# Root sums of the second gated layer moved between two products of a unit, and the next pass's input sums queued behind the global tile's first piece

## The chip, the cores and the metric

The kernel runs on one core of one Trainium2 chip. The metric is the device time in microseconds (us), of one execution from start to end. Three runs of the kernel before took 894.93, 897.28 and 897.6 us.

## What is computed

2304 tokens (4 batches of 512 local and 32 global tokens) go through attention, a feed-forward layer with ELU, and a gated feed-forward layer behind an RMS norm:

```python
x = np.ascontiguousarray(attn_out.transpose(0, 2, 1, 3)).reshape(B * S, H * D)
x = _moe_ref(x=x, **moe_kwargs)               # elu(x @ w_in) @ w_out
return _moe2_ref(x=x, **moe2_kwargs)

rms = np.sqrt(np.mean(x * x, axis=-1, keepdims=True) + 1e-06)
xn = x / rms * rms_g
g = xn @ w_gate
silu = g * (1.0 / (1.0 + np.exp(-g)))
val = xn @ w_val
return (silu * val @ w_out).astype(np.float32)
```

Model width 512, hidden width 1536 in the gated layer. The change concerns the gated layer and the end of the layer before it.

## The kernel before, in words

**Number format.** A large product takes both operands as a rounded high part and the rest (tile element 0 and 1), and sums three matmuls of the parts (`PASSES`). So every operand has a split: ScalarE (ACT) casts the high part, VectorE (DVE) subtracts it from the source. L625 and L626 do this for a group of weights (`split`), L691 and L692 for an input set (`x_split`), L828 and L829 for a gated result (`halves`).

**Who sets the order.** TensorE (PE) runs its instructions in the order of the program text. ACT and DVE are ordered by a scheduler; each then works its queue in that order. `behind(mark)` tells the scheduler to place what stands inside it after the two instructions that `mark` holds at that moment, one on ACT and one on DVE.

**End of the first layer.** `moe_block(3, slot3)` runs 16 steps j. A step has 12 matmuls h (L132), for j from 10 on also the products of the 128 global tokens (`hg` L701, transposes `egt` L708, `yg` L717), and 12 matmuls y (L153). From j=10 on `second_slot(j - 10)` prepares the gated layer's first pass: `y_square`, `y_root` (one matmul with a matrix of ones, L660; on ACT a table load and the square root, L662; on DVE the reciprocal, L663), `y_norm` (L670), `y_sums` (L676, L689) and `x_split`. h, hg and the two `ms` of this pass take turns in the two PSUM buffers of the pool `hps`.

**The gated layer.** Two passes k of 1024 tokens, each with 6 units i of hidden columns. The gate and value products of a unit go by a scheme with seven products in place of eight: positions 0 to 6, each for gate (z=0) and value (z=1), 6 matmuls per half, so 12 per position (L818). Positions 0, 2, 4, 5 add up in `A` (two buffers of `hps`), 1 and 3 with 6 in `Q` (two buffers of `aps`). ACT copies `A` out (L1006, L1019, L1025), DVE adds `Q` to the copies (`add_to`, L833). The results go into output products o (L824), 12 matmuls for one hidden block.

After a unit of pass 0 stands work for later: after unit 0 `g_root` (the root for the global tokens: a matmul `msg` L767, ACT's root L768, and their normed and split input `xg`, `xd`), after units 2 and 3 `y_root(1, ...)`, which take a buffer of `aps` as `Q` does.

**Between the passes.** Pass 0 ends with 12 output products of 12 matmuls (loop z over `js`). Between them lies the global tile in six pieces: `tile_products` (24 matmuls `pg`, L788; then silu on ACT, L793, and the product `pe` on DVE, L794), `tile_turn` (PE transposes `pe` to `pgt`, L800; ACT and DVE split it, L802 and L803), `tile_out` (6 matmuls `og`, L810). The same stretch makes the next pass's input: three wide sums (`y_sums`, L676), a fourth (L689) and seven input sets (`x_split`).

Of the kernel before, what the change touches and what calls it, by code (L numbers as in the profile page):

```python
# [7 lines left out]
F32 = mybir.dt.float32  # L8
# [4 lines left out]
AF = mybir.ActivationFunctionType  # L13
ALU = mybir.AluOpType
# [7 lines left out]
P = 128  # L22
# [11 lines left out]
def f(ap):  # L34
    return ap.bitcast(F32)
# [7 lines left out]
def fused_kernel(ctx: ExitStack, tc: tile.TileContext, kq, vl, gkq, gv, w_in, w_out, w_gate, w_val, w_o2, rms_g, consts, out):  # L43
# [533 lines left out]
        fetch()  # L577

    wraws, n_fetch, todo, groups = [], [0], [], {}
    n_split = [0]  # L580

    todo += [("w", q) for q in range(3)] + [("o", 0), ("o", 1)]
    for q in range(3, 54):
# [26 lines left out]
    def split(n=1):  # L610
        for _ in range(n):
            if n_split[0] >= len(todo):
                return
            kind, i = todo[n_split[0]]
            n_split[0] += 1
            raw = wraws.pop(0)
            if kind == "w":
                t = wpool.tile([P, 8, 2, P], F32R, tag="w", name="wS")
                raw = raw.rearrange("p (a n) -> p a n", a=8)
                groups[i] = t  # L620
            else:
                t = wpool.tile([P, 2, 2, 512], F32R, tag="w", name="wB")
                raw = raw.rearrange("p (a n) -> p a n", a=2)
                Wo[2 * i], Wo[2 * i + 1] = t[:, 0], t[:, 1]
            nc.scalar.copy(t[:, :, 0, :], raw)  # L625
            nc.vector.tensor_tensor(out=t[:, :, 1, :], in0=raw, in1=f(t[:, :, 0, :]), op=ALU.subtract)  # L626
            fetch()

    def need(q):
# [25 lines left out]

    def y_root(k, h):
        if k < 2:
            pool, tag = (aps, "att") if k else (hps, "h")
            ms = pool.tile([P, 512], F32, tag=tag, name="ms")
            nc.tensor.matmul(ms, bpools["ones"], rs_[k, h], start=True, stop=True)  # L660
            rs = stg.tile([P, 512], F32, tag="stg", name="rs")
            nc.scalar.activation(rs, ms, AF.Sqrt, bias=eps, scale=1.0 / DM)  # L662
            nc.vector.reciprocal(rs, rs)  # L663
            rs_[k, h] = rs
# [65 lines left out]
    def second_slot(i):  # L730

        if i == 0:
            y_square(0, 0)
        elif i == 1:
            y_root(0, 0)
            y_square(0, 1)
        elif i == 2:
            y_root(0, 1)
            y_norm(0, 0)
        elif i == 3:  # L740
            y_norm(0, 1)
            y_sums(0)
            split()
        elif i == 4:
            x_split(0, ("B11", "B21", "T2"))
        elif i == 5:
            split()
            x_split(0, ("T1", "T3"))
            with behind(mark):
                x_split(0, ("T4", "B22"))  # L750

    gg = {}

# [25 lines left out]
    def tile_products(i):  # L779
        ps = hps.tile([P, 512], F32, tag="h", name="pg")  # L780
        for h in range(2):
            need(21 + 2 * i + h + 1)
            w = groups[21 + 2 * i + h].rearrange("p (s a) l n -> p s a l n", a=2)
            xs_ = (xg[:, 0:2], xd if h else xg[:, 2:4])
            for m in range(2):
                for c in range(2):
                    for z, (xl, wl) in enumerate(PASSES):
                        nc.tensor.matmul(ps[:, 256 * h:256 * h + 256], xs_[m][:, c, xl, :], w[:, 2 * m:2 * m + 2, c, wl, :],  # L788
                                         start=(m == 0 and c == 0 and z == 0), stop=(m == 1 and c == 1 and z == 2))
        pv = ps.rearrange("p (h s n) -> p h s n", h=2, s=2)  # L790
        e = moe.tile([P, 512], F32, tag="e", name="pe", bufs=2)
        e2 = e[:, :256].rearrange("p (h n) -> p h n", h=2)
        nc.scalar.activation(e2, pv[:, :, 0, :], AF.Silu)  # L793
        nc.vector.tensor_tensor(out=e2, in0=e2, in1=pv[:, :, 1, :], op=ALU.mult)  # L794
        return e

    def tile_turn(i, e):
# [198 lines left out]
    for k in range(2):  # L996
# [3 lines left out]
        for i in range(6):  # L1000
            j1, j2 = 4 * (i // 2) + i % 2, 4 * (i // 2) + i % 2 + 2
            A = [hps.tile([P, 512], F32, tag="h", name="A") for _ in range(2)]
            t1, t2, t3 = (moe.tile([P, 2, 512], F32, tag=f"xT{z}", name=f"t{z + 1}") for z in range(3))
            for z in range(2):
                product(A[z], k, i, 0, z)
                nc.scalar.copy(t1[:, z], A[z])  # L1006
            Q = [aps.tile([P, 512], F32, tag="att", name="Q") for _ in range(2)]
            for z in range(2):
                product(Q[z], k, i, 1, z)
                add_to(t1[:, z], Q[z])  # L1010
                if z == 0:
                    nc.scalar.activation(t1[:, 0], t1[:, 0], AF.Silu)
            nc.vector.tensor_tensor(out=t1[:, 0], in0=t1[:, 0], in1=t1[:, 1], op=ALU.mult)
            p11 = halves(t1[:, 0])
            if late is not None:
                o_mm(os1, *late, False, False)
            for z in range(2):
                product(A[z], k, i, 2, z, False)
                nc.scalar.copy(t2[:, z], A[z])  # L1019
            Q = [aps.tile([P, 512], F32, tag="att", name="Q") for _ in range(2)]  # L1020
            for z in range(2):
                product(Q[z], k, i, 3, z)
            for z in range(2):
                product(A[z], k, i, 4, z, False)
                nc.scalar.copy(t3[:, z], A[z])  # L1025
                add_to(t3[:, z], Q[z])
                if z == 0:
                    nc.scalar.activation(t3[:, 0], t3[:, 0], AF.Silu)
            nc.vector.tensor_tensor(out=p2[:, slot2(j2), :], in0=t3[:, 0], in1=t3[:, 1], op=ALU.mult)
            o_mm(os1, p11, j1, i == 0, False)  # L1030
            for z in range(2):
                product(A[z], k, i, 5, z, False)
            e = moe.tile([P, 512], F32, tag="e", name="s", bufs=2)
            nc.scalar.activation(e, A[0], AF.Silu)
            nc.vector.tensor_tensor(out=e, in0=e, in1=A[1], op=ALU.mult)
            p21 = halves(e)
            for z in range(2):
                product(Q[z], k, i, 6, z, False)
                add_to(t2[:, z], Q[z])
                if z == 0:  # L1040
                    nc.scalar.activation(t2[:, 0], t2[:, 0], AF.Silu)
            kept = p2[:, slot2(j1), :] if i < 5 else t2[:, 0]
            nc.vector.tensor_tensor(out=kept, in0=t2[:, 0], in1=t2[:, 1], op=ALU.mult)
            late = (p21, j2)
            if k == 0 and i == 0:
                g_root(*yg)
                y_load(1)
            elif i == 1:
                y_square(k + 1, 0)
            elif i == 2:  # L1050
                y_root(k + 1, 0)
                y_square(k + 1, 1)
            elif i == 3:
                y_root(k + 1, 1)
                y_norm(k + 1, 0)
            elif i == 4:
                y_norm(k + 1, 1)
        js = [2, 0, 9, 3, 1, 6, 4, 7, 5, 10, 8, 11]
        second = lambda j: kept if j == 9 else p2[:, slot2(j), :]
# [3 lines left out]
        copied = store_out(os1, 8 * k, more)  # L1063
        ps.append(halves(second(js[1])))
        if k == 0:
            need(22)
            with behind(mark):
                pe = tile_products(0)
        os2 = [aps.tile([P, 512], F32, tag="att", name="o4") for _ in range(2)] + [yps.tile([P, 512], F32, tag=f"y{t}", name="o5") for t in range(2)]
        if k == 0:  # L1070
            og = yps.tile([P, 512], F32, tag="y3", name="og")
            with behind(mark):
                y_sums(1)
            pg = None
            for z, j in enumerate(js):
                o_mm(os2, ps.pop(0) if ps else halves(second(j)), j, z == 0, z == 11)
                if z % 2 == 0:
                    if z:
                        tile_out(og, z // 2 - 1, pg)
                    pg = tile_turn(z // 2, pe)  # L1080
                elif z < 11:
                    pe = tile_products(z // 2 + 1)
                if z % 3 == 1 and z < 9:
                    with behind(mark):
                        x_split(1, XSETS[z - 1:z + 2])
            tile_out(og, 5, pg)
            store_out(os2, 4)
            store_out([og], 16)
        else:
            for z, j in enumerate(js[:8]):  # L1090
                o_mm(os2, ps.pop(0) if ps else halves(second(j)), j, z == 0, False)
            rest = [(halves(second(j), f"xT{z}"), j) for z, j in enumerate(js[8:])]
            for t in range(4):
                for p, j in rest:
                    o_mm(os2, p, j, False, j == js[-1], (t,))
            store_out(os2, 12)
# [86 lines left out]
```

## Time and profile before

| what | value |
|---|---|
| median of three runs | 897.28 us (894.93 to 897.6) |
| the profiled execution, its own time | 896.46 us |
| its span, first to last instruction | 894.7 us |
| PE busy in the span | 859.4 us (96%) |
| DVE busy | 569.7 us (64%) |
| ACT busy | 449.8 us (50%) |
| granted TensorE clock, mean | 0.996 |

Busy time of PE counts matmuls with modelled ends, so the start times of instructions say more than their durations. Of the kernel's 40 equal slices all but the first few and the last show PE at 9 or 8 tenths.

### The profile page before, as it was taken

What the parts mean: (1) busy time and instruction counts of PE and PEld (TensorE: products, weight loads), DVE (VectorE), ACT (ScalarE), POOL (GpSimd) and SP (SyncE); (2) the same over time, 40 slices, a digit from 0 to 9 for tenths busy, and PEclk for the clock granted to TensorE, in tenths of its full rate; (3) what the DMA queues carried; (4) which work ended last, traced back from release to release, by engine and by line L of the source; (5) the groups of instructions that cost most, each with busy time, mean ns of one, the idle gap of its engine ahead of it and who ended that gap; (6) DMA issues with size and microseconds to landing.
All of it is one profiled execution on the core that took longest, in us unless ns stands there. A gap on an engine that the chain in (4) does not pass through costs nothing.

```text
span 894.7 us, 15197 instructions
## 1 busy us (share of the span) xinstructions
PE 859.4 (96%) x6238; PEld 695.3 (78%) x6238; DVE 569.7 (64%) x987; ACT 449.8 (50%) x753; POOL 16.2 (2%) x16
## 2 busy tenths in 40 slices
PE   4689999999999999999999999999989999999998
PEld 3567877888888888677878878788868888888886
DVE  3899988787777764543487775775575355444441
ACT  4667665555564544333454774555454344444430
POOL 0000000000000000000110010100000000000000
PEclk9999999999999999999999999999999999999999
DMA  9776375876678743441500842222333422221011
GB/s 360 299 284 209 124 270 178 292 268 184 233 261 280 232 169 112 158 167 60 191 1 24 290 133 71 71 71 78 111 118 95 142 82 70 72 94 48 1 47 48
DMA packets 58649, 134.16 MB, mean 150 GB/s; under 512 B 4820, under 2 KB 26836, under 8 KB 56020
## 3 DMA queue, kind: packets, MB, share of 16 engines
q1 hardware_dynamic: 58580, 133.19, 43.0%
q8 instruction: 49, 0.80, 0.4%
q14 instruction: 20, 0.16, 0.1%
HBM read 110.36 MB, written 22.81 MB: 149 GB/s over the span
## 4 chain that ended last, share of the span: by engine, by line
PE 79%; DVE 11%; ACT 4%; DMA 3%; issue 2%; POOL 0%; SPq 0%; ACTq 0%; DVEq 0%
PE y L153 15%; PE h L132 15%; PE o L824 14%; PE A L818 13%; PE Q L818 10%; PE pg L788 2%; DMA raw<-in_moe_w_in 2%; DVE dx L92 1%; DVE dx L93 1%; PE ptp L270 1%; PE s L242 1%; PE o L283 1%; DVE wA L99 1%; PE hg L701 1%; PE og L810 1%
## 5 line engine op out<-in xcount | busy, mean ns | idle before, releaser
L153 PE MATMUL y<-g,wA 128*128 128x512 f32 x768 | 197.1, 400 | 4.5 <-DVE g L140 3.8
L132 PE MATMUL h<-xT,wA 128*128 128x512 f32 x768 | 186.7, 392 | 2.8 <-DVE xT L308 1.8
L153 PEld LDWEIGHTS y<-g,wA 128*128 128x128 f32 x768 | 140.1, 189 | 39.6 <-issue 5.3
L132 PEld LDWEIGHTS h<-xT,wA 128*128 128x128 f32 x768 | 143.5, 188 | 34.5 <-DVE xT L308 2.4
L818 PE MATMUL A<-xc,wS 128*128 128x512 f32 x576 | 139.5, 391 | 0.0
L824 PE MATMUL o<-wB,p 128*128 128x512 f32 x576 | 138.9, 394 | 0.0
L818 PEld LDWEIGHTS A<-xc,wS 128*128 128x128 f32 x576 | 108.0, 188 | 23.3 <-issue 0.7
L824 PEld LDWEIGHTS o<-wB,p 128*128 128x128 f32 x576 | 108.4, 190 | 22.4
L818 PE MATMUL Q<-xc,wS 128*128 128x512 f32 x432 | 103.8, 389 | 0.0
L818 PEld LDWEIGHTS Q<-xc,wS 128*128 128x128 f32 x432 | 81.1, 188 | 16.8
L626 DVE TENSOR_TENSOR wS<-wraw,wS 128x1024 fp32r<-128x1024 f32 x54 | 65.7, 1222 | 44.0 <-ACT wS L625 44.0
L833 DVE TENSOR_TENSOR t<-t,Q 128x512 f32<-128x512 f32 x72 | 49.0, 683 | 45.3 <-ACT t L1025 23.0
L121 ACT ACTIVATE e<-h 128x512 f32<-128x512 f32 x48 | 28.9, 603 | 78.5 <-PE h L132 78.5
L625 ACT CAST wS<-wraw 128x1024 fp32r<-128x1024 f32 x54 | 56.3, 1050 | 22.5 <-PE Q L818 12.3
L139 ACT CAST g<-e 128x512 fp32r<-128x512 f32 x64 | 39.7, 621 | 50.0 <-DVE e L123 31.9
L123 DVE SCALAR_TENSOR_TENSOR e<-e,h 128x512 f32<-128x512 f32 x48 | 32.5, 677 | 34.4 <-ACT e L122 34.4
L140 DVE TENSOR_TENSOR g<-e,g 128x512 fp32r<-128x512 f32 x64 | 43.9, 686 | 12.0 <-ACT g L139 11.6
L83 ACT ACTIVATE dx<-raw 128x1024 f32<-128x1024 f32 x34 | 38.9, 1147 | 10.3 <-DMA raw<-in_moe_w_in 3.2
L92 DVE SCALAR_TENSOR_TENSOR dx<-raw,dx 128x1024 int32<-128x1024 int32 x34 | 42.1, 1246 | 0.7
L93 DVE SCALAR_TENSOR_TENSOR dx<-raw,dx 128x1024 int32<-128x1024 int32 x34 | 41.4, 1220 | 0.3
L90 DVE TENSOR_SCALAR dx<-dx 128x1024 f32<-128x1024 f32 x34 | 23.4, 689 | 25.2 <-ACT dx L83 25.2
L122 ACT ACTIVATE e<-e 128x512 f32<-128x512 f32 x48 | 30.5, 635 | 1.3
(199 smaller groups left out, 882.1 us busy)
## 6 DMA issues: line engine op xcount, KB each, us to landing
wraw<-wS SPq DMA_DIRECT2D x45, 512.0 KB, 3.3
raw<-in_moe_w_out SPq DMA_DIRECT2D x14, 1024.0 KB, 6.7
raw<-in_moe_w_in SPq DMA_DIRECT2D x8, 1024.0 KB, 8.2
raw<-in_moe_w_gate SPq DMA_DIRECT2D x6, 1024.0 KB, 5.8
raw<-in_moe_w_val SPq DMA_DIRECT2D x6, 1024.0 KB, 5.9
wS<-raw SPq DMA_DIRECT2D x48, 128.0 KB, 2.1
gvr<-in_gv SPq DMA_DIRECT2D x8, 640.0 KB, 4.2
wS<-dx SPq DMA_DIRECT2D x36, 128.0 KB, 2.5
```

Of the source, the lines that this page charges most:

```text
L83: ins = nc.scalar.activation(x, f(words(raw)[:, :, 1]), AF.Abs)
L92: nc.vector.scalar_tensor_tensor(out=i32(x), in0=word[:, :, 1], scalar=-0x40000000, in1=i32(x), op0=ALU.bitwise_and, op1=ALU.bitwise_or)
L93: nc.vector.scalar_tensor_tensor(out=i32(x), in0=word[:, :, 0], scalar=29, in1=i32(x), op0=ALU.logical_shift_right, op1=ALU.bitwise_or)
L132: nc.tensor.matmul(h[:, :n], W1[c, G][:, ws, o:o + P], xT[c][:, xs, :n], start=(k == 0), stop=(k == 11))
L139: hi = nc.scalar.copy(g[:, 0, :n], e[:, :n])
L140: mark[:] = hi, nc.vector.tensor_tensor(out=g[:, 1, :n], in0=e[:, :n], in1=f(g[:, 0, :n]), op=ALU.subtract)
L153: nc.tensor.matmul(ys[dc][:, :n], W2[j][:, ws, dc * P:(dc + 1) * P], g[:, gs, :n], start=(j == 0 and k == 0), stop=(j == 15 and k == 2))
L625: nc.scalar.copy(t[:, :, 0, :], raw)
L626: nc.vector.tensor_tensor(out=t[:, :, 1, :], in0=raw, in1=f(t[:, :, 0, :]), op=ALU.subtract)
L818: nc.tensor.matmul(ps, w[:, 2 * (q % 4) + c, ws, :], x[:, c, xs, :], start=(first and c == 0 and z == 0), stop=(c == 1 and z == 2), skip_g ...
L824: nc.tensor.matmul(os_[t], p[:, pp, t * P:(t + 1) * P], Wo[j][:, ww, :], start=(first and z == 0), stop=(last and z == 2))
L833: nc.vector.tensor_tensor(out=t, in0=t, in1=ps, op=ALU.add)
```

## The change

Five edits. The `ms` of the first pass take a buffer of `aps` in place of `hps`. In `second_slot` the split of T3 goes behind the mark of step 5. `g_root` and the two `y_root(1, ...)` move from the end of units 0, 2 and 3 to the place between the gate and the value half of position 2 of units 1, 2 and 3; the norms follow a unit earlier. Before the first piece of the global tile one more weight group is asked for behind it, and `y_sums(1)` and the input sets are placed behind the piece's `pe` (through `mark`) and behind the last weight split (`wmark`). The seven input sets go one to each z from 0 to 6 in place of three, three and one at z = 1, 4 and 7.

```diff
-    n_split = [0]
+    n_split, wmark = [0], []
...
-            nc.scalar.copy(t[:, :, 0, :], raw)
-            nc.vector.tensor_tensor(out=t[:, :, 1, :], in0=raw, in1=f(t[:, :, 0, :]), op=ALU.subtract)
+            hi = nc.scalar.copy(t[:, :, 0, :], raw)
+            wmark[:] = hi, nc.vector.tensor_tensor(out=t[:, :, 1, :], in0=raw, in1=f(t[:, :, 0, :]), op=ALU.subtract)
...
-            pool, tag = (aps, "att") if k else (hps, "h")
-            ms = pool.tile([P, 512], F32, tag=tag, name="ms")
+            ms = aps.tile([P, 512], F32, tag="att", name="ms")
...
-            x_split(0, ("T1", "T3"))
+            x_split(0, ("T1",))
             with behind(mark):
-                x_split(0, ("T4", "B22"))
+                x_split(0, ("T3", "T4", "B22"))
...
-        nc.scalar.activation(e2, pv[:, :, 0, :], AF.Silu)
-        nc.vector.tensor_tensor(out=e2, in0=e2, in1=pv[:, :, 1, :], op=ALU.mult)
+        act = nc.scalar.activation(e2, pv[:, :, 0, :], AF.Silu)
+        mark[:] = act, nc.vector.tensor_tensor(out=e2, in0=e2, in1=pv[:, :, 1, :], op=ALU.mult)
...
             for z in range(2):
                 product(A[z], k, i, 2, z, False)
                 nc.scalar.copy(t2[:, z], A[z])
+                if z == 0:
+                    if k == 0 and i == 1:
+                        g_root(*yg)
+                    elif i in (2, 3):
+                        y_root(k + 1, i - 2)
...
             if k == 0 and i == 0:
-                g_root(*yg)
                 y_load(1)
             elif i == 1:
                 y_square(k + 1, 0)
             elif i == 2:
-                y_root(k + 1, 0)
                 y_square(k + 1, 1)
+                y_norm(k + 1, 0)
             elif i == 3:
-                y_root(k + 1, 1)
-                y_norm(k + 1, 0)
-            elif i == 4:
                 y_norm(k + 1, 1)
...
         if k == 0:
-            need(22)
             with behind(mark):
+                need(22)
                 pe = tile_products(0)
+                need(24)
...
-            with behind(mark):
+            with behind(mark), behind(wmark):
                 y_sums(1)
...
-                if z % 3 == 1 and z < 9:
-                    with behind(mark):
-                        x_split(1, XSETS[z - 1:z + 2])
+                if z < 7:
+                    with behind(mark), behind(wmark):
+                        x_split(1, XSETS[z:z + 1])
```

On PE, from the first product of unit 1 on; before:

```order
L818 MATMUL A<-xc,wS 128x512 x12
L818 MATMUL Q<-xc,wS 128x512 x12
L767 MATMUL msg<-acc,ones 128x128
L818 MATMUL A<-xc,wS 128x512 x12
L818 MATMUL Q<-xc,wS 128x512 x12
```

and after (the first A and Q are positions 5 and 6 of unit 0; line numbers of the changed kernel are lower by one here):

```order
L817 MATMUL A<-xc,wS 128x512 x12
L817 MATMUL Q<-xc,wS 128x512 x12
L817 MATMUL A<-xc,wS 128x512 x12
L817 MATMUL Q<-xc,wS 128x512 x12
L823 MATMUL o_5354<-wB,p 128x512 x3
L823 MATMUL o_5355<-wB,p 128x512 x3
L823 MATMUL o_5356<-wB,p 128x512 x3
L823 MATMUL o_5357<-wB,p 128x512 x3
L817 MATMUL A<-xc,wS 128x512 x6
L766 MATMUL msg<-acc,ones 128x128
L817 MATMUL A<-xc,wS 128x512 x6
L817 MATMUL Q<-xc,wS 128x512 x12
```

`msg` stands no longer right behind unit 0's last Q but three products later, between the halves of A. The `ms` of units 2 and 3 move in the same way.

On DVE, at the end of pass 0, from the split of the second output product's operand on; before:

```order
L829 TENSOR_TENSOR p<-p_5353,p 128x512
L676 TENSOR_TENSOR tt<-yb 128x1024
L626 TENSOR_TENSOR wS<-wraw,wS 128x8x128 x2
L676 TENSOR_TENSOR yb<-yb,ya 128x1024
L626 TENSOR_TENSOR wS<-wraw,wS 128x8x128
L692 TENSOR_TENSOR xc<-ya,xc 128x2x512 x2
L794 TENSOR_TENSOR pe<-pe,pg 128x256
L676 TENSOR_TENSOR tt<-yb 128x1024
```

and after:

```order
L828 TENSOR_TENSOR p<-p_5353,p 128x512
L626 TENSOR_TENSOR wS<-wraw,wS 128x8x128 x2
L793 TENSOR_TENSOR pe<-pe,pg 128x256
L675 TENSOR_TENSOR tt<-yb 128x1024
L691 TENSOR_TENSOR xc<-ya,xc 128x2x512
L626 TENSOR_TENSOR wS<-wraw,wS 128x8x128
L675 TENSOR_TENSOR yb<-yb,ya 128x1024
L828 TENSOR_TENSOR p<-t_6228,p 128x512
L802 TENSOR_TENSOR pg<-pgt,pg 128x256
L828 TENSOR_TENSOR p<-p_5353,p 128x512
L675 TENSOR_TENSOR tt<-yb 128x1024
L793 TENSOR_TENSOR pe<-pe,pg 128x256
```

Two wide sums, a weight split and two input splits stood between the operand split and the first `pe`; now two weight splits do, and the sums and input splits follow it, spread over the pieces.

## Rows read from the trace of the kernel before

**Rows 1.** Page, part 1: busy us (share of the span) and instructions of each engine.

```profile
PE 859.4 (96%) x6238; PEld 695.3 (78%) x6238; DVE 569.7 (64%) x987; ACT 449.8 (50%) x753; POOL 16.2 (2%) x16
```

**Rows 2.** Waits of PE: line waited for: us in total, times, longest us.

```profile
PE pgt L800 <- DVE pe L794: 4.1, 1, 4.1
```

**Rows 3.** Timeline, first piece: start us, us, engine line op out<-in xcount [idle before <-releaser].

```profile
648.17 2.35 DVE L626 TENSOR_TENSOR wS<-wraw,wS 128x1024 fp32r<-128x1024 f32 x2
648.43 2.91 PE L824 MATMUL o<-wB,p 128*128 128x512 f32 x12
...
651.03 0.38 ACT L793 ACTIVATE pe<-pg 128x256 f32<-128x256 f32 x1
...
652.71 2.35 DVE L692 TENSOR_TENSOR xc<-ya,xc 128x1024 fp32r<-128x1024 f32 x2
654.98 0.41 DVE L794 TENSOR_TENSOR pe<-pe,pg 128x256 f32<-128x256 f32 x1
...
655.45 0.44 PE L800 MATMUL pgt<-ident,pe 128*128 128x128 f32 x2 [4.11 <-DVE pe L794]
...
660.08 2.31 PE L788 MATMUL pg<-wS,xg 128*128 128x256 f32 x18
```

**Rows 4.** Timeline, the second piece, PE only.

```profile
662.95 2.91 PE L824 MATMUL o<-wB,p 128*128 128x512 f32 x12
...
665.69 1.53 PE L810 MATMUL og<-wB,pg 128*128 128x512 f32 x6
...
667.06 0.38 PE L800 MATMUL pgt<-ident,pe 128*128 128x128 f32 x2
...
670.05 2.31 PE L788 MATMUL pg<-wS,xg 128*128 128x256 f32 x18
```

**Rows 5.** Stretch table: us, PE, PEld, DVE, ACT, POOL busy (instructions), PEclk, DMA share, GB/s.

```profile
655.00:660.00 5.00, 4.55 (x14) 3.64 (x15) 4.82 (x8) 3.31 (x4) 0.00 (x0) 0.66 0.14 47
```

**Rows 6.** Timeline, end of unit 0 and start of unit 1.

```profile
504.76 0.59 ACT L1019 COPY t<-A 128x512 f32<-128x512 f32 x1
...
513.12 2.88 PE L818 MATMUL Q<-xc,wS 128*128 128x512 f32 x12
...
517.64 0.49 PE L767 MATMUL msg<-acc,ones 128*128 128x128 f32 x2 [1.64 <-DVE t L833]
...
518.27 1.28 ACT L768 ACT_TABLE_LOAD   x1
...
519.57 0.37 ACT L768 ACTIVATE acc<-msg,cst 128x128 f32<-128x128 f32 x1
...
520.73 2.88 PE L818 MATMUL Q<-xc,wS 128*128 128x512 f32 x12
```

**Rows 7.** Chain that ended last, one position's 12 matmuls: start us, us, what.

```profile
520.90 2.72 PE Q L818 x12
```

**Rows 8.** Timeline, first layer's step 12 and start of step 13.

```profile
460.44 1.02 PE L660 MATMUL ms<-acc,ones 128*128 128x512 f32 x2
...
462.54 3.02 PE L132 MATMUL h<-xT,wA 128*128 128x512 f32 x12 [1.09 <-DVE e L115]
...
465.40 0.60 PE L708 MATMUL egt<-ident,e 128*128 128x128 f32 x4
```

**Rows 9.** Timeline, the roots after units 2 and 3.

```profile
567.50 1.10 PE L660 MATMUL ms<-acc,ones 128*128 128x512 f32 x2 [0.37 <-DVE t L833]
...
569.34 0.69 ACT L662 ACTIVATE rs<-ms,cst 128x512 f32<-128x512 f32 x1
...
570.06 3.35 DVE L663 RECIPROCAL rs<-rs 128x512 f32<-128x512 f32 x1 [0.70 <-ACT rs L662]
...
592.97 1.02 PE L660 MATMUL ms<-acc,ones 128*128 128x512 f32 x2
...
596.59 2.88 PE L818 MATMUL Q<-xc,wS 128*128 128x512 f32 x12
```

**Rows 10.** Timeline, wait of ACT for an input of the next pass.

```profile
500.34 0.63 ACT L647 ACTIVATE acc<-ya 128x512 f32<-128x512 f32 x1 [2.22 <-DMA yT<-yev]
```

## The prediction

> **What bounds the kernel now.** First the busy shares: PE is busy for 96% of the span [rows 1], so time can only come off where PE stands still or runs slowly. Then PE's own waits. Between the start of the gated layer's preparation and the second pass the trace shows four: 4.11 us for `pe` [rows 2, 3], 1.64 us before `msg` [rows 6], 1.09 us before a product h [rows 8] and 0.37 us before an `ms` [rows 9]. The change touches all four. Then the stretch table around the longest: behind it the granted clock is 0.66 as a mean over 5 us [rows 5], so PE ran for a part of that stretch at the lower of its two levels, and the wait costs more than its length. I therefore take no idle time as a price, but the distance between two starts on PE, in a stalled place and in an undisturbed one. One position of 12 matmuls takes 2.72 us [rows 7].
>
> **The global tile's first piece.** PE starts the output product behind the first `pg` at 648.43 and the second `pg` at 660.08 [rows 3]: 11.65 us for two output products and a `pgt`. In the second piece the same stretch runs from 662.95 to 670.05 and holds an `og` besides, 665.69 to 667.06 [rows 4]: 7.10 - 1.37 = 5.73 us. The difference, 11.65 - 5.73 = **5.92 us**, is wait and slow clock together. The cause is the DVE queue: `pe` stands behind weight and input splits and runs at 654.98 [rows 3], while its silu on ACT started at 651.03, itself behind two input casts. Changed, DVE has two weight splits (2.35 us from 648.17 [rows 3], and the sum that now stands ahead of them moves away) and then `pe`. Even if they began no earlier, `pe` would start at 650.52 and end by 650.93; PE wants it one output product after 648.43, at about 648.43 + 2.72 = 651.15. On ACT two weight casts stand ahead of the silu in place of three and two input casts, so it can run as soon as `pg` is through. So all of it goes, but the margin by rows is only some 0.2 us, near 1 us if the splits move up by the 1.2 us of the sum in front of them. Bounds: 5.92 and, if the clock is kept but a short wait stays, about 4.9.
>
> **What the piece now carries instead.** The sums and seven input splits do not vanish. Per piece DVE gets two weight splits and two input splits, 2.35 + 2.35 = 4.70 us, and at most one sum, 1.2 us (an estimate: half of the two weight splits, equal in size [rows 3]). The pieces follow at 670.05 - 660.08 = 9.97 us [rows 3, 4]. The cover is PE's own work: `pe` is wanted an output product and an `og` after its `pg`, 2.72 + 1.37 = 4.1 us, and only what the order puts between the last piece's `pg` split and `pe` can delay it: an operand split and, once each, a sum. Cost nothing; if that cover went, a piece would lose up to the 5.92 us of the first. Asking for one more weight group early costs nothing either: its cast stood in the queue before. No DMA is added; the fetches follow the weight splits, the first two of which come earlier, and the third later by about a sum and an input split, 2.4 us, of a weight that is wanted a whole piece later. The seven input sets are through one z earlier than before (z = 6, not 7), and T3 of the first pass, now behind step 15's split, is wanted only at position 4 of unit 0, four positions into the layer.
>
> **`msg`.** From the last Q of unit 0 at 513.12 to the first Q of unit 1 at 520.73 pass 7.61 us [rows 6], for two positions and `msg`. `msg` takes a buffer that Q uses and waits until DVE's sum has read it. `msg` and a position together take 520.73 - 517.64 = 3.09 us, so `msg` alone 0.37. Undisturbed it is 2 x 2.72 + 0.37 = 5.81 us: gain **1.80 us**. Without `msg`, Q of unit 1 still needs that buffer, but only a position later, 2.72 us after the old request, more than the 1.64 us that it was late. In its new place `msg` finds a buffer that was read long before. Bounds: 1.80, and 1.4 if Q inherits a rest.
>
> **`ms` of the first pass.** With four takers on the two buffers of `hps`, the h of step 13 gets hg's buffer and must wait for its ELU; with `ms` elsewhere it gets that of the h before. `ms`, h and the start of the transposes run from 460.44 to 465.40, 4.96 us [rows 8]; an `ms` and 12 matmuls undisturbed from 592.97 to 596.59, 3.62 us [rows 9]. Gain **1.34 us**. The new buffer in `aps` is free: the transposes of the step before were read by then. What is late next is a transfer: ACT waits 2.22 us for a load of the second pass [rows 10], and the copies of A queue behind it. That load is issued when the last split of the first pass is through, which follows PE, so I let it come earlier too; the lower bound of this term is 0.5.
>
> **`ms` of units 2 and 3.** The wait of **0.37 us** before the first [rows 9] goes; the second had none. The matmuls themselves stay and cost what they did. Moved, a root has the third next half of a product behind it that wants its buffer. For `msg` that is 0.37 + 2.72 = 3.09 us after `msg` starts (the second half of A and the first of Q make one position); ACT needs a copy of 0.59, the table load of 1.28 and the root of 0.37, sum 2.24 us [rows 6]. For an `ms`, 3.62 [rows 9] against 0.59 + 1.28 + 0.69 = 2.56 us [rows 6, 9]. So both fit, with 0.85 and 1.06 us to spare, less what the handovers take. DVE's reciprocal of 3.35 us and the norms now stand ahead of a unit's sums with Q; PE wants Q's buffers again two positions and an output product later, about 8 us, so nothing is late.
>
> The table load takes 1.28 us and the next instruction on ACT starts 1.30 us after it [rows 6]. The Trainium skill, ScalarE: Activation LUTs, section "What ACT_TABLE_LOAD costs", puts a switch at 2.66 us, the load and a drain of 1.38. By that figure `msg` would hold Q for about 0.5 us and each `ms` for 0.3, an estimate from that page, and the sum below would be 1.1 us smaller. The trace shows the load but no drain, and I go by it.
>
> **Sum.** 5.92 + 1.80 + 1.34 + 0.37 = 9.43 us. The profiled execution took 896.46 us: 887.0. The median of the three runs is 897.28, 0.8 higher, so I forecast **887.8 us**. About 0.3%, 2.7 us, is what a measurement can tell from no change.
>
> **Rivals.**
> *The roots hold Q.* ACT may have another piece of work between copy and root (a weight cast of about the length of a copy and more, or a square). If each of the three roots came later by another table load, 1.28 us, and the slack were gone, PE would lose 3 x 1.28 = 3.8 us: 891.6. For it: the slack is below 1.1 us. Against it: the only thing the order puts there is the copy. The drain that the page tells of would be a smaller form of this. Chance 0.10.
> *Only the tile gains.* The stretch from unit 0 to `msg` may go by its transfers [rows 10]; then what the first layer and `msg` give is waited away, and 5.92 + 0.37 stay: 897.28 - 6.29 = 891.0. Against it: the waits of PE there end on DVE, not on a transfer. Chance 0.11.
> *The first piece still waits.* `pe` needs ACT and DVE both in time, with a margin of 0.2 to 1 us. If the weights came late, the wait would stand and 1.80 + 1.34 + 0.37 = 3.5 us be left: 893.8. Chance 0.06.
> *Slower: the wait comes back in the later pieces.* If the sums and splits now queued between the pieces hold `pe` for longer than its 4.1 us of cover, each piece that carries them can stall as the first did. Three pieces at 5.92 are 17.8 us, against 9.4 gained: 905.6; from two stalled pieces on it is a loss. Against it: 5.9 us of new work in 9.97 us, and `pe` ahead of it in the queue. Chance 0.04.
>
> **Chances and range.** The forecast itself has 0.69. Its low end is 897.28 - 9.43 and another 2.35 us, by which the lowest of the three runs lay below their median: 885.5. The upper end takes in the bounds of the terms (1.0 + 0.4 + 0.8 = 2.2 us less, 890.0) and the first two rivals: 892.0. The third and the fourth stay outside. Faster by over 0.3%: 0.69 + 0.10 + 0.11 and half of the third rival, which lies at that edge but for a run's scatter, less 0.03 for something unseen: 0.90. Same: the other half and as much again, 0.05. Slower: the fourth and a little for what I don't see, 0.05.
>
> **What would show it.** `pgt` of the first piece without a wait for `pe`, no clock below 1.0 behind it, and `pg` to `pg` near 5.7 us for that stretch; `msg` inside position 2 of unit 1 and Q behind it without a wait for ACT; the h of step 13 right behind `ms`. I am wrong if PE waits for `pe` or `pg` in a later piece, or for ACT's root behind `msg` or `ms`, or if PE's starts near 518 did not come earlier.

## The result, and the profile after

The changed kernel takes 886.72 us (median of four runs, 885.89 to 887.41) against 897.28: a ratio of 0.9888 with a 95% interval of 0.9869 to 0.9906. 887.8 had been forecast. The profiled execution took 886.63 us with a span of 884.8, 9.8 us below that of before.

The waits of PE in the whole span, longest first (line waited for: us in total, times, longest us):

```profile
PE s L236 <- ACT masks L420: 6.9, 1, 6.9
PE s L242 <- DMA kq<-in_kq: 3.9, 2, 3.7
PE y L153 <- DVE g L140: 3.3, 2, 2.6
```

These three, and the shorter ones below them in that list, lie in the first 300 us, which the change leaves alone. The waits for `pe` [rows 2, 3], before `msg` [rows 6], before h [rows 8] and before `ms` [rows 9] are gone. The line numbers are one lower than before in this part.

The first piece of the global tile, against [rows 3]; timeline, columns as there:

```profile
643.44 2.36 DVE L626 TENSOR_TENSOR wS<-wraw,wS 128x1024 fp32r<-128x1024 f32 x2 [0.24 <-ACT wS L625]
...
644.50 2.91 PE L823 MATMUL o<-wB,p 128*128 128x512 f32 x12
...
644.70 0.38 ACT L792 ACTIVATE pe<-pg 128x256 f32<-128x256 f32 x1 [0.35 <-PE pg L787]
...
645.72 0.41 DVE L793 TENSOR_TENSOR pe<-pe,pg 128x256 f32<-128x256 f32 x1
...
647.25 0.38 PE L799 MATMUL pgt<-ident,pe 128*128 128x128 f32 x2
...
650.24 2.32 PE L787 MATMUL pg<-wS,xg 128*128 128x256 f32 x18
```

From output product to second `pg` it is now 650.24 - 644.50 = 5.74 us, where 11.65 were. `pe` ends at 646.13, 1.12 us before PE turns it. And the clock, against [rows 5] (columns as there):

```profile
645.00:650.00 5.00, 5.00 (x24) 4.09 (x23) 5.00 (x6) 2.87 (x5) 0.00 (x0) 1.00 0.64 213
650.00:655.00 5.00, 5.00 (x35) 4.61 (x34) 4.10 (x7) 2.31 (x4) 0.00 (x0) 1.00 0.32 105
```

PE is busy without a gap and the granted clock stays at 1.00, the upper of its two levels.

The global tokens' root in its new place, against [rows 6]; timeline of PE and ACT:

```profile
511.70 2.88 PE L817 MATMUL Q<-xc,wS 128*128 128x512 f32 x12
...
517.14 2.88 PE L817 MATMUL Q<-xc,wS 128*128 128x512 f32 x12
...
522.58 1.52 PE L817 MATMUL A<-xc,wS 128*128 128x512 f32 x6
...
523.95 0.38 PE L766 MATMUL msg<-acc,ones 128*128 128x128 f32 x2
...
524.20 0.59 ACT L1018 COPY t<-A 128x512 f32<-128x512 f32 x1 [1.35 <-PE A L817]
524.80 1.28 ACT L767 ACT_TABLE_LOAD   x1
...
525.56 2.90 PE L817 MATMUL Q<-xc,wS 128*128 128x512 f32 x12
526.10 0.37 ACT L767 ACTIVATE acc<-msg,cst 128x128 f32<-128x128 f32 x1
```

The last Q of unit 0 and the first of unit 1 are 5.44 us apart, two positions and nothing else. A position with `msg` inside runs from 522.58 to 525.56, 2.98 us, so `msg` costs 0.26. The second half of Q, half of 2.72 us after 525.56 and so at about 526.9, finds the root done at 526.47.

Step 12 of the first layer, against [rows 8]:

```profile
460.31 1.02 PE L659 MATMUL ms<-acc,ones 128*128 128x512 f32 x2
460.76 3.33 PE L132 MATMUL h<-xT,wA 128*128 128x512 f32 x12
...
463.93 0.60 PE L707 MATMUL egt<-ident,e 128*128 128x128 f32 x4
```

`ms` to transposes is 3.62 us in place of 4.96; h stands right behind `ms`.

**A measure with less scatter.** The start of the kernel shifts all that follows by up to some four us from run to run: the first `ms` starts between 446.39 and 450.32 in the profiles below. So I compare traces also by the stretch from the first `ms` of the first pass (L660 or L659) to the first product A of the second pass, where all of the change lies. Before it runs from 448.16 to 711.29, 263.13 us; after from 448.03 to 701.44, 253.41 us: 9.72 us less. From there to the end of the span it is 183.4 us in both.

### The profile page after: what moved, and what is told of

Its sections match the earlier page's. It is cut to its first block, busy times and chain, and to the rows that moved or that the text cites. A ratio compares the mean times of both kernels' runs of the same rounds, so it can differ in the third digit from the quotient of the medians.

```text
span 884.8 us, 15201 instructions
## 1 busy us (share of the span) xinstructions
PE 859.4 (97%) x6238; PEld 696.3 (79%) x6238; DVE 570.8 (65%) x987; ACT 449.1 (51%) x753; POOL 15.8 (2%) x16
## 4 chain that ended last, share of the span: by engine, by line
PE 85%; DVE 7%; DMA 4%; ACT 2%; issue 1%; SPq 1%; ACTq 0%
PE y L153 16%; PE h L132 16%; PE o L823 15%; PE A L817 15%; PE Q L817 11%; PE pg L787 2%; DMA kq<-in_kq 2%; DMA raw<-in_moe_w_in 2%; PE s L242 1%; PE o L283 1%; PE yg L716 1%; PE hg L700 1%; DVE dx L92 1%; PE ptp L270 1%; DVE dx L93 1%
```

## The experiments

Ten kernels, in three jobs. The kernel before was timed in each job too: 896.40, 895.66 and 896.41 us. The third column is the stretch, with its difference from the changed kernel's 253.41. It comes from one trace of each kernel. Two kernels in whose stretch PE waits for nothing, third weight split and two bundles, lie within 0.05 us of the changed kernel. The times tell less: of the slower kernels only tile back, tile alone and no mark at pe have an interval clear of the changed kernel's. For the others the argument rests on the traces.

| kernel | us (ratio to before, 95% interval) | stretch, us |
|---|---|---|
| changed | 886.72 (0.9888, 0.9869 to 0.9906) | 253.41 |
| ms back | 888.19 (0.9904, 0.9889 to 0.9920) | 254.72, +1.31 |
| msg back | 888.43 (0.9909, 0.9893 to 0.9924) | 255.24, +1.83 |
| tile back | 891.83 (0.9951, 0.9938 to 0.9964) | 259.26, +5.85 |
| tile alone | 889.51 (0.9923, 0.9910 to 0.9936) | 256.68, +3.27 |
| third weight split | 885.52 (0.9877, 0.9845 to 0.9908) | 253.46, +0.05 |
| sums ahead | 888.55 (0.9911, 0.9880 to 0.9942) | 255.41, +2.00 |
| roots later | 890.12 (0.9930, 0.9903 to 0.9957) | 257.74, +4.33 |
| two bundles | 886.84 (0.9890, 0.9863 to 0.9917) | 253.45, +0.04 |
| no mark at pe | 893.26 (0.9961, 0.9946 to 0.9976) | 260.21, +6.80 |
| mark only | 888.43 (0.9907, 0.9891 to 0.9924) | 257.08, +3.67 |

### Undo one part

*ms back* in the changed kernel:

```diff
-            ms = aps.tile([P, 512], F32, tag="att", name="ms")
+            pool, tag = (aps, "att") if k else (hps, "h")
+            ms = pool.tile([P, 512], F32, tag=tag, name="ms")
```

> The changed kernel with the first pass's two ms back in the buffers of hps. Theory (four waits that each go by themselves): h of step 13 waits for DVE's e<-hg again, ms to transposes 4.96 us in place of 3.62, the time 1.3 us above the changed kernel's 886.7: 888.0. Rival (the gain there is waited away at the later load of the next pass's input): the wait is back in the trace, but the start of the second pass and the time stay within 0.3 us of the changed kernel's.

*msg back*:

```diff
                 if z == 0:
-                    if k == 0 and i == 1:
-                        g_root(*yg)
-                    elif i in (2, 3):
+                    if i in (2, 3):
                         y_root(k + 1, i - 2)
...
             if k == 0 and i == 0:
+                g_root(*yg)
                 y_load(1)
```

> The changed kernel with the global tile's root back behind unit 0. Theory: PE waits for DVE's sum with Q before msg, the last Q of unit 0 to the first Q of unit 1 takes 7.6 us again in place of 5.4, the time is 1.8 us up: 888.5. Rival (the wait came from the weight transfers, which now start 1.3 us earlier beside a PE that is as early): the wait before msg is below 0.5 us and the time within 0.5 us of 886.7.

*tile back*: the five lines on the tile, from `mark` in `tile_products` to the input sets, as before.

> The changed kernel with the end of the first pass as before (weight group asked for outside, no mark at the tile's product pe, sums and splits three, three and one). Theory: PE waits about 4.1 us for pe and runs at the lower clock behind it; output product to second pg 11.6 us in place of 5.74; the time 5.9 us up: 892.6. Rival (the clock's share does not hang on this wait): 4.1 us up, 890.8, with the granted clock at 1.0 behind the wait.

The waits come back one by one. In turn the timelines of ms back, msg back and tile back:

```profile
464.70 3.04 PE L132 MATMUL h<-xT,wA 128*128 128x512 f32 x12 [1.08 <-DVE e L115]
```

```profile
516.63 0.49 PE L766 MATMUL msg<-acc,ones 128*128 128x128 f32 x2 [1.65 <-DVE t L832]
```

```profile
650.41 0.44 PE L799 MATMUL pgt<-ident,pe 128*128 128x128 f32 x2 [4.11 <-DVE pe L793]
```

They are as long as before, also beside a PE that is otherwise earlier, and the stretches give back 1.31, 1.83 and 5.85 us. So the rival of ms back, by which the gain would be waited away at a later load, falls, and so does the rival of msg back, which expected a wait below 0.5 us. In tile back the clock behind the wait is again 0.66 over 5 us:

```profile
650.00:655.00 5.00, 4.59 (x14) 3.68 (x15) 4.83 (x8) 3.31 (x4) 0.00 (x0) 0.66 0.13 45
```

With 4.11 us of wait and 5.85 of loss, 1.7 us are left beyond the wait. Most of that is the slow clock: a wait of 1.84 us without a lower clock behind it (sums ahead, below) cost only 0.16 us beyond its length. So the rival of 4.1 us falls.

### One part alone

*tile alone* is the kernel before with the same five places on the tile, and `wmark`, as in the change.

> The kernel before with the end of the first pass alone as in the change. Theory: the terms add, so 5.9 us below the kernel before's 897.3: 891.4, and the waits before msg (1.6 us), before h of step 13 (1.1 us) and before the ms of unit 2 (0.4 us) stand as before. Rival (the tile needs the earlier roots and norms to be in time): a wait for pe of over 0.5 us remains and the time is above 892.5.

The stretch is 263.13 - 256.68 = 6.45 us shorter than before, not 5.9, and no wait for `pe` is left, so the tile needs no other part of the change. The time, 889.51, is 1.9 us below the expectation, which set out from 897.3; beside it the kernel before took 896.40. The 0.5 us too much in the stretch have a place: the wait before `msg` is 1.18 us here and was 1.64. The kernel before first, then tile alone:

```profile
512.95 1.05 ACT L625 CAST wS<-wraw 128x1024 fp32r<-128x1024 f32 x1 [1.57 <-DMA wraw<-wS]
```

```profile
511.99 1.05 ACT L625 CAST wS<-wraw 128x1024 fp32r<-128x1024 f32 x1 [0.84 <-DMA wraw<-wS]
...
516.68 0.49 PE L767 MATMUL msg<-acc,ones 128*128 128x128 f32 x2 [1.18 <-DVE t L833]
```

A weight cast ahead of it on ACT waits 0.84 us for its transfer here. In the kernel before the same cast waited 1.57, in msg back 1.54 beside a wait of 1.65 before `msg`. The tile's edits work some 130 us later and do not explain this. In these three traces, then, `msg` waits longer where the transfer lands later; that a part of its old wait hung on the transfer fits them, but no run varied the transfer alone.

### How much stands ahead of pe

*third weight split*: `need(25)` in place of `need(24)`.

> The changed kernel with a third weight split ahead of the first pe (one more weight group asked for). Theory (pe is limited by DVE's queue, with 1.1 us to spare in the changed kernel's trace): the third split costs 1.2 us of that, pe ends within 0.2 us of the moment PE wants it, a wait of 0 to 0.3 us, the time within 0.4 us of 886.7. Rival (the margin is smaller than the trace shows, since handovers add): a wait of over 0.5 us and 887.3 or more.

*sums ahead*: `need(25)` and `y_sums(1)` placed between `need(22)` and `tile_products(0)`, under the same `behind(mark)`.

```diff
                 need(22)
+                need(25)
+                y_sums(1)
                 pe = tile_products(0)
-                need(24)
...
-            with behind(mark), behind(wmark):
-                y_sums(1)
```

> The changed kernel with two of the wide sums and a third weight split ahead of the first pe, but no input split. Theory: pe ends some 2.2 us after PE wants it and PE waits so long. If the clock stays (as behind the 1.6 us wait before msg in the kernel before), the time is 2.2 us up, 888.9, and output product to second pg takes about 8.0 us. If the clock falls behind this wait too, as behind the 4.1 us one, up to 1.8 us more: 890.7.

*no mark at pe*:

```diff
-        act = nc.scalar.activation(e2, pv[:, :, 0, :], AF.Silu)
-        mark[:] = act, nc.vector.tensor_tensor(out=e2, in0=e2, in1=pv[:, :, 1, :], op=ALU.mult)
+        nc.scalar.activation(e2, pv[:, :, 0, :], AF.Silu)
+        nc.vector.tensor_tensor(out=e2, in0=e2, in1=pv[:, :, 1, :], op=ALU.mult)
```

> The changed kernel without the mark at the tile's product pe, so that sums and input sets follow only the last operand split and the last weight split. Theory (the mark at pe is what moves pe ahead): two sums, two input splits and a weight split stand between the two weight splits and pe, five of about 1.2 us, so pe comes some 4.7 us too late, the clock falls behind the wait, and the time is 6 to 7 us up: 893. Rival (the early request of weights and the mark at the weight split carry the gain): no wait for pe over 0.5 us, 886.7.

With a third split PE does not wait, so the margin holds one more operation of 1.2 us, with 0.06 us to spare (`pe` ends at 646.19, PE turns it at 646.25); the time, 885.52, cannot be told from the changed kernel's, whose interval overlaps. With two sums and a third split PE waits 1.84 us and the stretch grows by 2.00; without the mark two sums, two input splits and a weight split come between, PE waits 4.45 us and the stretch grows by 6.80. Timelines, sums ahead first, then no mark:

```profile
647.10 0.41 DVE L793 TENSOR_TENSOR pe<-pe,pg 128x256 f32<-128x256 f32 x1
...
647.57 0.44 PE L799 MATMUL pgt<-ident,pe 128*128 128x128 f32 x2 [1.84 <-DVE pe L793]
```

```profile
651.67 0.41 DVE L793 TENSOR_TENSOR pe<-pe,pg 128x256 f32<-128x256 f32 x1
...
652.14 0.69 PE L799 MATMUL pgt<-ident,pe 128*128 128x128 f32 x2 [4.45 <-DVE pe L793]
```

The mark at `pe` is what takes the wait away; the early weight request and the mark at the weight split without it leave all of it.

The traces can also be put in a row by what stands on DVE between the operand split and the first `pe`. With 2 operations of 1.2 us (changed), 3 (third weight split), 5 (sums ahead) and 7 (the kernel before), `pe` ends 1.63, 2.76, 4.69 and 6.96 us after the start of the output product, and PE waits 0, 0, 1.84 and 4.11 us. No mark at pe has 7 too, with 7.30 and 4.45 us. That is about 1.1 us for each operation, be it a sum, a weight split or an input split.

### What the later pieces bear

*two bundles*:

```diff
-                if z < 7:
+                if z in (1, 3):
                     with behind(mark), behind(wmark):
-                        x_split(1, XSETS[z:z + 1])
+                        x_split(1, XSETS[:4] if z == 1 else XSETS[4:])
```

> The changed kernel with the seven input splits in two bundles, four behind the second piece and three behind the third. Theory (spreading them is not needed, only that none stands ahead of a piece's own pe; the pieces give 9.97 us each): no wait for pe or a weight split over 0.4 us, the time within 0.5 us of 886.7. Rival (a bundle of 4.9 us beside two weight splits of 2.4 us and the operand splits overruns the piece): waits for pe, a weight split or an operand split of 1 us or more in the second or third piece, 888 or more.

*mark only*: as tile back, but with the mark at `pe` kept.

> The changed kernel with the end of the first pass as before but for the mark at pe: weight groups asked for as before, input sets three, three and one. Theory: three weight splits stand ahead of pe, as in the run with a third weight split, which left no wait; the sums and bundles of three follow pe; no wait over 0.4 us, the time within 0.6 us of 886.7. Rival (each of the other edits takes a part of the wait away): a wait for pe, an operand or a weight split of 0.6 us or more at the tile, 887.5 or more.

Two bundles leave no wait: spreading the sets one by one is not needed where each bundle follows its own piece's `pe`. My expectation for mark only fell. The first piece is in time, but PE waits 1.84 us in the third:

```profile
654.72 2.36 DVE L691 TENSOR_TENSOR xc<-ya,xc 128x1024 fp32r<-128x1024 f32 x2 [0.52 <-ACT xc L690]
...
661.00 1.22 DVE L688 TENSOR_TENSOR ya<-ya,tt 128x1024 f32<-128x1024 f32 x1
...
665.34 1.22 DVE L691 TENSOR_TENSOR xc<-ya,xc 128x1024 fp32r<-128x1024 f32 x1
666.47 2.36 DVE L626 TENSOR_TENSOR wS<-wraw,wS 128x1024 fp32r<-128x1024 f32 x2
668.75 0.42 DVE L793 TENSOR_TENSOR pe<-pe,pg 128x256 f32<-128x256 f32 x1
...
669.22 0.44 PE L799 MATMUL pgt<-ident,pe 128*128 128x128 f32 x2 [1.84 <-DVE pe L793]
```

Both bundles of three, the fourth sum and four weight splits stand between two `pe` on DVE, some 13 us at 1.2 us each, in a piece of 9.97. At z = 4 the mark holds an operand split and not the piece's `pe`. In the program text that split comes after `pe`, but on DVE it runs at 660.40, 8 us ahead of it, so the second bundle slips in ahead of `pe`. That is the mechanism of the forecast's slower rival, in one piece: +3.67 us. With the further edits of the change it does not happen; which of them it takes was not tried apart.

### Where the root stands

*roots later*: `if z == 1` in place of `if z == 0` ahead of the roots in position 2.

> The changed kernel with the three roots behind both halves of position 2, one half of a product later, so that Q wants their buffer a half sooner. Theory (copy, table load of 1.28 us and root are all that stands on ACT): Q waits about 0.9 us behind msg and 0.6 us behind each ms, 2.1 us in all, 888.8. Rival (a switch of tables costs 2.66 us): 1.4 us more for each, 6.2 us in all, 892.9. Other rival (Q does not want that buffer): no wait, 886.7.

The stretch grows by 4.33 us, between theory (2.1) and rival (6.2). The trace tells why; timeline around `msg`, PE and ACT:

```profile
524.00 0.38 PE L766 MATMUL msg<-acc,ones 128*128 128x128 f32 x2
...
524.20 0.59 ACT L1018 COPY t<-A 128x512 f32<-128x512 f32 x1 [0.72 <-PE A L817]
524.68 1.05 ACT L625 CAST wS<-wraw 128x1024 fp32r<-128x1024 f32 x1
525.75 1.28 ACT L767 ACT_TABLE_LOAD   x1
...
527.05 0.37 ACT L767 ACTIVATE acc<-msg,cst 128x128 f32<-128x128 f32 x1
...
527.47 1.66 PE L817 MATMUL Q<-xc,wS 128*128 128x512 f32 x6 [1.69 <-ACT acc L767]
```

The scheduler put a weight cast of 1.05 us between copy and load here, and at the second of the two `ms` as well, but not at the first. PE waited 1.69 us here and, in the same trace, 0.42 and 1.37 us behind the two `ms`:

```profile
553.57 1.66 PE L817 MATMUL Q<-xc,wS 128*128 128x512 f32 x6 [0.42 <-ACT rs L661]
```

```profile
580.61 1.67 PE L817 MATMUL Q<-xc,wS 128*128 128x512 f32 x6 [1.37 <-ACT rs L661]
```

The waits sum to 3.48 us. By distance, from the first A of position 2 to the first A of position 4, the three places take 1.96, 0.71 and 1.67 us more than in the changed kernel, which is the whole 4.33. The theory had 0.9, 0.6 and 0.6: it was short by about one cast in the two places that have one, and by 0.1 in the other. So the rival of 2.66 us for a switch falls; the table load is 1.28 us and the root follows 1.30 after its start. The first step of the forecast's first rival, another piece of work between copy and root, is real, but in this other order; and that Q wants the root's buffer is shown.

## Why the prediction was right

**The sum.** 9.43 us off the profiled execution were forecast; its own difference is 9.83, the stretch's 9.72. By terms, forecast and found: first piece 5.92 and 11.65 - 5.74 = 5.91 us; `msg` 1.80 and 7.61 - 5.44 - 0.26 = 1.91; `ms` of the first pass 1.34 and 4.96 - 3.62 = 1.34; the `ms` of units 2 and 3 the rest, 9.72 - 9.16 = 0.56, where only the wait of 0.37 was counted. Undone one by one, the first three gave back 5.85, 1.83 and 1.31, so they add up and none hides another. The measured 886.72 lies 1.1 us below the forecast of 887.8. Of this the sum accounts for 0.4. The other 0.7 is scatter: the forecast added the 0.8 us by which the median of the kernel before lay above its profiled execution, and in the changed kernel that difference is 0.1.

**Prices by distance, not by idle time.** The four waits sum to 7.2 us in the page's idle time. Taking the distance of starts in a stalled and an undisturbed place brought in the slow clock behind the longest wait, about 1.7 us, and tile back showed it. The smallest term was the exception: the forecast took the idle 0.37 us as its price. By distance, from the Q ahead of the first `ms` to the Q behind it, it is 571.21 - 564.25 = 6.96 us before. Two positions are 5.44, and an `ms` between them costs 3.62 - 2.72 = 0.90 [rows 7, 9]. That leaves 0.62 us, close to the rest above.

```profile
564.25 2.88 PE L818 MATMUL Q<-xc,wS 128*128 128x512 f32 x12
...
571.21 2.88 PE L818 MATMUL Q<-xc,wS 128*128 128x512 f32 x12
```

**The margin of the first piece.** 0.2 to 1 us were forecast and 1.12 found, just above the upper end. The two weight splits start 644.50 - 643.44 = 1.06 us ahead of the output product, where it was 648.43 - 648.17 = 0.26 [rows 3]. So they moved up by 0.80 us and not by the whole sum of 1.2, because they now wait for ACT's cast (0.24 us). What stood ahead of `pe` before were seven operations by the listing of that order: two sums, three weight splits (the sentence under the listing says one) and two input splits. The third weight split used the margin up without a wait.

**Only the tile gains.** This rival fell, but its mechanism was there: ACT started on the next pass's input only 500.34 - 499.37 = 0.97 us earlier, though it was ready for it 1.47 us earlier, and waited 2.72 us for the load in place of 2.22 [rows 10].

```profile
499.37 0.63 ACT L647 ACTIVATE acc<-ya 128x512 f32<-128x512 f32 x1 [2.72 <-DMA yT<-yev]
```

PE still did not wait for anything behind it.

**The root's slack.** The forecast gave 0.85 us for `msg` less handovers; root done at 526.47 and Q's half at about 526.9 leave 0.4. The claim that the order puts only the copy there held in the changed kernel, and fell in roots later. From the start of the load to the root it is 1.30 us. The Trainium skill, ScalarE: Activation LUTs, section "What ACT_TABLE_LOAD costs", counts a drain of 1.38 us besides the load. No trace here shows it: wherever ACT's next instruction waits for nothing, it starts within 0.05 us of the load's end.

**The later pieces.** The cover held in the changed kernel and in two bundles. The forecast's load for a piece did not come out in the first one: it had at most one sum in each, and all three wide sums ran between the first `pe` and the second, at 646.04, 649.45 and 652.12. It cost nothing, because there only an operand split and the last sum stood between the `pg` split and `pe`, as the forecast had it, and `pe` waited 0.39 us for ACT and not for DVE's queue; it ended 3.1 us before PE turned it:

```profile
653.73 0.42 DVE L793 TENSOR_TENSOR pe<-pe,pg 128x256 f32<-128x256 f32 x1 [0.39 <-ACT pe L792]
...
657.23 0.38 PE L799 MATMUL pgt<-ident,pe 128*128 128x128 f32 x2
```

Mark only showed that the slower rival's mechanism can happen: one piece overrun cost 3.67 us.

Two things stayed untried. The edit that moves T3's split was not run alone; no wait stands near it before or after. And the `ms` of units 2 and 3 were not put back alone, so their term rests on the distances in the traces.

## What to carry to other kernels

Price a stall as the distance between two starts in the stalled place, less the same distance in an undisturbed one: that takes in what the clock does afterwards. Where an engine waits for a short operation, look at what the scheduler put ahead of it in its queue, and tie the long, unhurried work behind that very operation; a mark on a neighbour lets it slip ahead. Then count, between two such operations, what the queue holds against the time that the waiting engine's own work gives.

## What the runs showed of the chip that was not expected

The same length of wait did not bring the same clock. In sums ahead PE waited 1.84 us at 647.57 and the clock stayed at 1.00; in mark only it waited 1.84 us at 669.22 and the clock fell to 0.66 over the 5 us behind. The stretch tables, sums ahead first:

```profile
645.00:650.00 5.00, 3.16 (x16) 2.30 (x15) 5.00 (x6) 0.99 (x2) 0.00 (x0) 1.00 0.86 297
650.00:655.00 5.00, 5.00 (x35) 4.62 (x34) 1.84 (x4) 1.92 (x4) 0.00 (x0) 1.00 0.05 16
```

```profile
665.00:670.00 5.00, 3.16 (x16) 2.34 (x15) 5.00 (x6) 2.25 (x5) 0.00 (x0) 1.00 0.22 79
670.00:675.00 5.00, 5.00 (x21) 4.17 (x20) 1.55 (x4) 0.69 (x2) 0.00 (x0) 0.66 0.74 236
```

So one wait cost 2.00 us in the stretch and the other 3.67, and the length of a wait alone does not say whether the lower level follows. Behind the wait of 4.45 us in no mark at pe the table shows 0.50 and then 0.81 over two stretches of 5 us, and behind 4.11 us in tile back 0.66 and 1.00. In roots later, behind waits of 1.69, 0.42 and 1.37 us, it stayed at 1.00. What decides it is open.
